# Strassen block products in the last channel products of an attention and MLP-mixer kernel

## The chip, the core and the metric

The kernel runs on one core of one Trainium2 chip. The metric is the device time of one execution in microseconds; lower is better. On the core the engines run side by side, each with a queue that it works off in order: PE (matrix products, with PEld loading the stationary operand), DVE (vector), ACT (scalar), POOL and SP, the last two here only issuing transfers.

## The reference

```python
scores = (q @ k.T) / sqrt(64)                    # q, k, v: 8 batches, 12 heads, 448 rows, 64 wide
attn = maximum(scores, 0) ** 2 / 448
x = (attn @ v) laid out as 8 x 448 x 768         # heads side by side
h = maximum(x.T @ w_tok1, 0) @ w_tok2            # mixing along the 448 rows, 256 wide inside
u = x + h.T
out = u + maximum(u @ w_ch1, 0) @ w_ch2          # the two channel products, 768 -> 1536 -> 768
```

Inputs and output are float32; the kernel multiplies in bf16 and accumulates in float32.

## The kernel before

**Steps.** A step s (0 to 23) is four heads of one batch, three steps to a batch. For each step q, k and v are loaded by POOL (`ld`), q and k are transposed (by PE for the first ten steps, later by a copy on DVE, `i`, and a transposing transfer of SP, `x`), and seven score blocks follow: `S{s}.{c}` on PE, two evictions with a rectifier `r` on ACT or DVE, a squaring `q` on DVE (L426), and the value product `V{s}.{c}` (L443), which adds up over the seven blocks. `xe` evicts it, `xd` transposes it by a transfer, `t1` and `rt`, then `t2` and `u` (L500, DVE) do the token mixing and leave a 128-channel slice of u in `uTs`, 6 x 896 columns for a pair of batches. `ub` (SP) transposes u a second time into `u_sbs`, for the residual at the end.

**Channel products.** For each batch b and each of twelve 128-column blocks e of w_ch1, `C1.{b}.{e}` is six matmuls of 448 columns in one of the eight PSUM banks (L521), evicted with a rectifier by ACT (`c1e`, L250) into `r2s`. For each pair of batches p and each of its seven 128-row tiles t, `C2.{p}.{t}.{i}` is twelve matmuls of 384 columns (L569) for each half i of the output row; DVE adds u (`c2e`, L576) into one of three output buffers, and SP stores the tile in two transfers (`st`, L559). The very last tile is made in three parts of 384, 256 and 128 columns.

**Order.** `ORDER` is one long list, written ahead of time, of every operation with its PSUM banks (a digit each) or its engine (A for ACT, D for DVE). Each engine works off its own operations in the order of this list, whatever becomes ready first; the framework adds the waits between engines, from the regions that instructions read and write. The list puts channel products of earlier batches between the score and value blocks, which alone would leave PE waiting for ACT and DVE.

**What the change touches.** The buffers (`raws`, `sides`, `kqTs`, `sqs`, `xTs`, `r1s`, `outs`), `channel2` (L544) with its stores, the loop over batches at the end (L595) and the part of `ORDER` from the last score blocks on.

Of the kernel before, what the change touches and what calls it, by code (L numbers as in the profile page):

```python
# [172 lines left out]
C1.5.4:3 c1e5.10:A q21.3:D q21.6:D t2.18.1:5 c1e5.4:A q22.4:D t1.19.0:2 u18.1:D V21.0:41 rt19.0:A ub6.1  # L173
S22.6:06 S23.0:73 V21.1 r22.6.0:A r22.6.1:D V21.2 S22.5:52 r23.0.0:A V21.3 r23.0.1:D S23.1:06 r22.5.0:A V21.4
r22.5.1:D V21.5 S23.2:73 r23.1.0:A V21.6 q23.0:D r23.1.1:A S23.3:52 C1.5.2:0 q22.5:D r23.2.0:A r23.2.1:A
r23.3.0:D r23.3.1:A t2.18.0:6 q23.1:D c1e5.2:A t2.19.1:7 q23.2:D C2.2.2.0:3 u18.0:D u19.1:D ub6.0 xe21.0:A
xe21.1:D q23.3:D C1.5.9:5 xd21 c2e2.2.0:D q22.6:D S22.2:20 c1e5.9:A S22.3:67 ub6.3 S22.0:41 r22.2.0:A
r22.2.1:D t1.20.0:3 r22.0.0:A r22.0.1:D r22.3.0:A C1.5.3:5 r22.3.1:D rt20.0:A q22.0:D t2.19.0:2 q22.2:D
c1e5.3:A V23.0:04 q22.3:D V22.0:16 V22.1 S23.6:73 u19.0:D V23.1 V23.2 r23.6.0:A V22.2 r23.6.1:D ub6.2 V22.3
S23.4:52 V22.4 q23.6:D V23.3 r23.4.0:A V22.5 S23.5:73 r23.4.1:A C2.2.1.0:5 r23.5.0:A r23.5.1:D q23.4:D q23.5:D  # L180
C1.5.0:2 c2e2.1.0:D t2.20.1:7 c1e5.0:A t2.20.0:3 u20.1:D V22.6 V23.4 u20.0:D V23.5 xe22.0:A ub6.5 V23.6
xe22.1:D C1.5.6:5 xe23.0:A xe23.1:D xd22 C1.6.8:2 c1e5.6:A ub6.4 t1.21.0:7 c1e6.8:A C1.6.0:3 rt21.0:A xd23
C1.5.8:1 c1e6.0:A C2.2.0.0:6 c1e5.8:A t1.22.0:0 c2e2.0.0:D C1.6.4:4 rt22.0:A C1.6.7:5 c1e6.4:A t1.23.0:2
c1e6.7:A t2.21.0:7 C1.5.1:3 u21.0:D ub7.0 t2.22.1:1 c1e5.1:A C1.6.2:6 u22.1:D ub7.3 C1.6.3:0 c1e6.2:A
t2.21.1:4 c1e6.3:A C1.6.11:5 u21.1:D ub7.1 rt23.0:A C1.5.11:7 c1e6.11:A t2.23.1:3 c1e5.11:A C1.6.1:1 u23.1:D
ub7.5 C2.2.1.1:6 c1e6.1:A t2.22.0:0 c2e2.1.1:D C1.6.10:4 u22.0:D st15.0 st15.64 t2.23.0:2 c1e6.10:A ub7.2
# [5 lines left out]
st22.64 C1.7.3:0 C2.2.3.0:4 c1e7.3:A C2.2.4.1:6 c2e2.3.0:D st17.0 st17.64 C2.2.6.1:7 c2e2.4.1:D st18.0 st18.64
C2.3.5.0:0 c2e2.6.0:D c2e2.6.1:D C2.3.2.0:4 st20.0 st20.64 c2e3.0.0:D c2e3.0.1:D C2.3.3.1:6 st21.0 st21.64
C2.3.3.0:1 c2e3.2.1:D c2e3.2.0:D st23.0 C2.3.4.0:7 st23.64 c2e3.3.0:D c2e3.3.1:D st24.0 C2.3.5.1:2 c2e3.4.0:D
st24.64 C2.3.4.1:3 c2e3.5.0:D c2e3.5.1:D st26.0 st26.64 C2.3.6.0:5 c2e3.4.1:D st25.0 st25.64 C2.3.6.1:4
c2e3.6.0:D st27.0.0 C2.3.6.2:1 st27.0.64 c2e3.6.1:D st27.1.0 c2e3.6.2:D st27.1.64 st27.2.0 st27.2.64
"""


# [1 line left out]
def kernel(ctx: ExitStack, tc: tile.TileContext, q: bass.AP, k: bass.AP, v: bass.AP, moe_w_tok1: bass.AP, moe_w_tok2: bass.AP, moe_w_ch1: bass.AP, moe_w_ch2: bass.AP, out: bass.AP):  # L201
    nc = tc.nc
    B, H, S, D = q.shape
# [20 lines left out]
    xTs = [sbuf.tile([128, 2, SP], BF16, name=f'xT{i}') for i in range(NX)]  # L224
# [23 lines left out]
    def relu(o, out, ps):  # L248
        if o.on == 'ACT':
            nc.scalar.activation(out, ps, AF.Relu)  # L250
# [293 lines left out]
    def channel2(bb, t):  # L544
        r2 = r2s[bb % 2]
        n = bb * NT + t
        out_sb = outs[n % NO]
        last = n == 4 * NT - 1
        parts = [(0, 3), (3, 5), (5, 6)] if last else [(0, 3), (3, 6)]
        rows = out[2 * bb:2 * bb + 2].rearrange('b (p c) m -> b c p m', c=KC)  # L550
        (b0, r0), (b1, r1) = (divmod(2 * t, KC), divmod(2 * t + 1, KC))
        pieces = [(slice(0, 64), rows[b0, r0]), (slice(64, 128), rows[b1, r1])]

        def store(name, cols, deps):
            for p, dst in pieces:
# [4 lines left out]
                w = 1.29 / len(pieces) * (cols.stop - cols.start) / DM  # L560
                st.setdefault(n, []).append(add(Op(f'st{name}.{p.start}', 'SP', emit_st, deps)))
        for i, (g0, g1) in enumerate(parts):
            cols = slice(g0 * 128, g1 * 128)
            size = (g1 - g0) * 128

            def emit(o, cols=cols, size=size):
                o.ps = bank(o, 0, 'm2_ps')
                for e in range(EC):
                    nc.tensor.matmul(o.ps[:, :size], lhsT=r2[:, e, t * 128:(t + 1) * 128], rhs=wc2[:, e, cols], start=e == 0, stop=e == EC - 1)  # L569
            deps = [c1e[2 * bb + h, e] for h in range(2) if (t <= HT if h == 0 else t >= HT) for e in range(EC)]  # L570
            deps += list(wc2_ops.values())
            u = Op(f'C2.{bb}.{t}.{i}', 'PE', emit, deps, banks=1)
            c2[bb, t, i] = add(u)

            def evict(o, u=u, cols=cols, size=size, g0=g0, g1=g1):
                nc.vector.tensor_tensor(out=out_sb[:, cols].rearrange('n (g d) -> n g d', d=128), in0=u.ps[:, :size].rearrange('n (g d) -> n g d', d=128), in1=u_sbs[bb % 2][:, g0:g1, t, :], op=ALU.add)  # L576
# [70 lines left out]
```

## Time and profile before

| | |
|---|---|
| median of 3 runs | 361.92 us (360.82 to 362.55) |
| span of the profiled execution | 360.1 us |
| its own time beside the span | not among the numbers; the median of the runs is 1.8 us above the span |
| PE busy | 351.5 us, 98% of the span |
| DVE, ACT busy | 243.8 and 190.0 us, 68% and 53% |
| mean granted TensorE clock | 0.994 of full speed |

The span runs from the first to the last instruction of the profiled execution. Busy time of an engine is the time in which at least one of its instructions ran; the durations of DVE and ACT instructions overlap by some tens of nanoseconds where they follow each other directly, so the distance between two starts, not the duration, is what one costs in a full queue. In a chain of waits, each piece is followed back to what released it.

### The profile page before, as it was taken

The numbers are of one execution on the slowest core, as the hardware profiler recorded it, in microseconds if no ns is written. First come the engines' busy times: TensorE is split into PE (matmuls) and PEld (weight loads), VectorE is DVE, ScalarE is ACT, GpSimd is POOL, SyncE is SP. The second block draws the span as 40 slices with busy tenths as digits, with TensorE's granted clock in tenths as the row PEclk, the third lists the DMA queues.
The fourth block names the chain that finished last, engine by engine and source line by source line (L and its number), as shares of the span: only waits on it lengthen the run. The fifth ranks groups of instructions, "written<-read, shape, count | busy, mean of one in ns | idle before, by whom it ended". The sixth has DMA issues, their size and how long they took to land.

```text
span 360.1 us, 8713 instructions
## 1 busy us (share of the span) xinstructions
PE 351.5 (98%) x3543; PEld 196.9 (55%) x3543; DVE 243.8 (68%) x457; ACT 190.0 (53%) x392; POOL 92.0 (26%) x157
## 2 busy tenths in 40 slices
PE   7799999999999999999999999999999999999995
PEld 3456555565555545655555555555556555555563
DVE  3999995978686898989986879788970211101342
ACT  3999996546654667537665637367644432110000
POOL 9985313530650333303330523010000000000000
PEclk9899999999999999999999999999999999999999
DMA  8999999999999989999999999974213231103555
GB/s 150 182 181 165 186 190 200 133 172 220 91 194 130 166 173 199 180 187 146 174 205 190 111 176 159 231 140 87 53 23 71 44 89 44 46 0 87 129 134 133
DMA packets 98297, 50.17 MB, mean 139 GB/s; under 512 B 71440, under 2 KB 94800, under 8 KB 98256
## 3 DMA queue, kind: packets, MB, share of 16 engines
q1 hardware_dynamic: 72880, 27.93, 45.2%
q0 software_dynamic: 25136, 21.47, 44.4%
q8 instruction: 28, 0.46, 0.5%
q10 hardware_dynamic: 240, 0.20, 0.2%
q14 instruction: 13, 0.11, 0.1%
HBM read 43.38 MB, written 11.01 MB: 151 GB/s over the span
## 4 chain that ended last, share of the span: by engine, by line
PE 93%; DVE 2%; ACT 2%; DMA 1%; issue 0%; SPq 0%
PE m_ps L521 31%; PE m_ps L569 31%; PE sc_ps L416 9%; PE acc_ps L443 9%; PE t_ps L487 6%; PE h_ps L496 5%; ACT sq L250 1%; DMA side<-in_q_dram 1%; PE kqT_ps L373 1%; DVE sq L426 1%; PE x_ps L478 1%; DVE sq L252 1%; DVE kqT L258 0%; ACT kqT L256 0%; SPq L325 0%
## 5 line engine op out<-in xcount | busy, mean ns | idle before, releaser
L250 ACT ACTIVATE sq<-sc_ps 128x448 bf16<-128x448 f32 x232 | 110.6, 570 | 29.7 <-PE sc_ps L416 28.5
L521 PE MATMUL m_ps<-uT_sb,wc 128*128 128x448 bf16 x576 | 118.7, 353 | 0.0
L569 PE MATMUL m_ps<-wc,r_sb 128*128 128x384 bf16 (+2 forms) x684 | 114.6, 323 | 0.0
L250 ACT ACTIVATE r_sb<-m_ps 128x448 bf16<-128x448 f32 x96 | 52.8, 551 | 88.5 <-PE m_ps L521 88.1
L426 DVE TENSOR_TENSOR sq<-sq 128x896 bf16<-128x896 bf16 x168 | 97.0, 617 | 0.6
L569 PEld LDWEIGHTS <-r_sb 128*128 128x128 bf16 x684 | 65.8, 98 | 45.8 <-issue 3.1
L521 PEld LDWEIGHTS <-wc 128*128 128x128 bf16 x576 | 54.5, 98 | 54.1 <-issue 7.3
L576 DVE TENSOR_TENSOR out_sb<-m_ps,u_sb 128x384 f32<-128x384 f32 (+2 forms) x57 | 30.9, 549 | 72.5 <-PE m_ps L569 65.2
L252 DVE TENSOR_SCALAR sq<-sc_ps 128x448 bf16<-128x448 f32 x104 | 60.6, 617 | 12.2 <-PE sc_ps L416 11.9
L272 POOL DMA_DIRECT2D v_raw<-in_v_dram x48 | 29.0, 608 | 121.4 <-PE sc_ps L416 76.7
L416 PE MATMUL sc_ps<-kqT 64*64 64x448 bf16 x672 | 54.7, 361 | 0.7 <-DVE kqT L258 0.2
L443 PE MATMUL acc_ps<-sq,v_raw 64*64 64x448 bf16 x672 | 49.2, 357 | 1.8 <-DVE sq L426 1.8
L500 DVE TENSOR_TENSOR uT_sb<-h_ps,xT 128x448 bf16<-128x448 f32 x48 | 28.8, 618 | 17.3 <-PE h_ps L496 17.2
L272 POOL DMA_DIRECT2D k_raw<-in_k_dram x48 | 29.4, 625 | 13.7 <-DMA wc<-in_moe_w_ch_dram 6.4
L416 PEld LDWEIGHTS <-kqT 64*64 64x64 bf16 x672 | 20.6, 107 | 20.3 <-issue 11.8
L272 POOL DMA_DIRECT2D q_raw<-in_q_dram x46 | 28.3, 629 | 7.4 <-PE m_ps L521 4.2
L443 PEld LDWEIGHTS <-v_raw 64*64 64x64 bf16 x672 | 20.9, 108 | 15.6 <-issue 6.7
L487 PE MATMUL t_ps<-x_sb,wt 128*128 128x256 bf16 (+1 forms) x216 | 25.4, 261 | 0.0
L250 ACT ACTIVATE r_sb<-t_ps 128x512 bf16<-128x512 f32 (+1 forms) x26 | 15.0, 584 | 19.1 <-PE t_ps L487 19.0
L496 PE MATMUL h_ps<-wt,r_sb 128*128 128x448 bf16 x96 | 24.3, 353 | 0.0
L487 PEld LDWEIGHTS <-wt 128*128 128x128 bf16 x216 | 18.9, 98 | 7.3 <-issue 1.8
L455 DVE TENSOR_SCALAR xT<-acc_ps 128x448 bf16<-128x448 f32 x24 | 14.7, 617 | 0.2 <-PE acc_ps L443 0.2
(35 smaller groups left out, 103.3 us busy)
## 6 DMA issues: line engine op xcount, KB each, us to landing
out_dram<-out_sb SPq DMA_DIRECT2D x54, 192.0 KB, 3.4
k_raw<-in_k_dram POOLq DMA_DIRECT2D x48, 112.0 KB, 6.1
v_raw<-in_v_dram POOLq DMA_DIRECT2D x48, 112.0 KB, 5.0
q_raw<-in_q_dram POOLq DMA_DIRECT2D x46, 112.0 KB, 6.6
wc<-in_moe_w_ch_dram POOLq DMA_DIRECT2D x6, 768.0 KB, 16.9
u_sb<-uT_sb SPq DMA_TRANSPOSE x48, 4.6
side<-in_q_dram SPq DMA_DIRECT2D x2, 224.0 KB, 3.8
kqT<-side SPq DMA_TRANSPOSE x28, 6.3
```

Of the source, the lines that this page charges most:

```text
L250: nc.scalar.activation(out, ps, AF.Relu)
L252: nc.vector.tensor_scalar(out=out, in0=ps, scalar1=0.0, scalar2=None, op0=ALU.max)
L272: nc.gpsimd.dma_start(out=raws[t][s % NR][64 * half:64 * (half + 1)], in_=src[b, h0:h0 + 2].rearrange('e (p c) d -> p e (c d)', c=KC))
L416: nc.tensor.matmul(o.ps[e][64 * half:64 * (half + 1), :S], lhsT=lhsT, rhs=rhs, start=True, stop=True, skip_group_check=True)
L426: sq_ops[s, c] = [add(Op(f'q{s}.{c}', 'DVE', lambda o: nc.vector.tensor_tensor(out=buf, in0=buf, in1=buf, op=ALU.mult), ev))]
L443: nc.tensor.matmul(o.ps[half][64 * e:64 * (e + 1), :S], lhsT=r[rows, e, c * D:(c + 1) * D], rhs=sq[rows, e, :], start=c == 0, stop=c == KC ...
L487: nc.tensor.matmul(o.ps[:, j, :], lhsT=wt1[:, c, j * 128:(j + 1) * 128], rhs=x_sb[:, p0:p1, c, :], start=c == 0, stop=c == 3)
L496: nc.tensor.matmul(o.ps[:, :S], lhsT=r1[:, j, a * 128:(a + 1) * 128], rhs=wt2[:, j, :], start=j == 0, stop=j == JC - 1)
L500: nc.vector.tensor_tensor(out=uTs[bb % 2][:, 2 * i + a, off:off + S].rearrange('n (c p) -> n c p', c=KC), in0=t2.ps[:, :S].rearrange('n (p ...
L521: nc.tensor.matmul(ps[:, :S], lhsT=wc1[:, g, e * 128:(e + 1) * 128], rhs=uT[:, g, off:off + S], start=g == 0, stop=g == CC - 1)
L569: nc.tensor.matmul(o.ps[:, :size], lhsT=r2[:, e, t * 128:(t + 1) * 128], rhs=wc2[:, e, cols], start=e == 0, stop=e == EC - 1)
L576: nc.vector.tensor_tensor(out=out_sb[:, cols].rearrange('n (g d) -> n g d', d=128), in0=u.ps[:, :size].rearrange('n (g d) -> n g d', d=128 ...
```

## The change

A matrix product in 2 x 2 blocks needs eight block products; Strassen's scheme (in Winograd's form) needs seven, and sums of blocks ahead of and behind them. The changed kernel uses it in two places. For the last pair of batches (p = 3) the first channel product is made of seven block products for each of six pairs of column blocks (`fast1`: `M1.3.{e}.{name}`, three matmuls of 448 columns each). For the last two pairs (p = 2 and 3), the second channel product is made so for the tiles t = 0, 1, 2 together with 4, 5, 6 (`fast2`: `M2.{p}.{t}.{name}`, six matmuls of 384 columns each, giving two tiles); tile 3 stays as it was.

New operations: `w2` and `w1`, sums of blocks of the two weights (8 of 128x1152 and 12 of 128x768 bf16, DVE); `tu`, sums of blocks of u (4 of 128x1344, DVE); `s1`, copies of a PSUM bank to float32 in SBUF (18, ACT), after which more is accumulated onto the same bank; `d1`, which join a copy and a bank (24 of 128x448, DVE); `z1`, the rectifier in place on 128x896 (12: 5 on DVE, 7 on ACT); `h2` and `h3`, sums of blocks of its result (24 each of 128x384 bf16, DVE); `d2`, which add u and the products into an output buffer (48 of 128x384, DVE, in place of 24 `c2e`). The `c1e` of the last two batches go (24, ACT). The sums lie in one large tile, `arena`, which the loads, transposes and squares of the attention use before, and the output buffers grow from three to five, two of them where `xTs` was. The order is unchanged up to `u18.1`, in the middle of the attention's last steps, and new from there.

```diff
+FAST1, FAST2 = ({3}, {2, 3})
+TILES = [*range(14), 14, 18, 15, 19, 16, 20, 17, 21, 25, 22, 26, 23, 27, 24]
...
 C1.5.4:3 c1e5.10:A q21.3:D q21.6:D t2.18.1:5 c1e5.4:A q22.4:D t1.19.0:2 u18.1:D
...
+w2.0.1:D t2.18.0:4 w2.0.0:D
+ub6.1 rt19.0:A t1.20.0:1 u18.0:D w2.1.0:D t2.19.1:0 ub6.0 rt20.0:A t2.19.0:6 u19.1:D V21.0:73 V21.1 u19.0:D
...
+tu3.3:D M1.3.0.1:6 M1.3.1.1:0 M1.3.1.5:5 s1.3.0.1:A M1.3.1.2:7 s1.3.1.1:A M1.3.0.2:4 M1.3.1.6 M1.3.0.6
...
+h3.2.2:D d2.2.1.22a:D d2.2.0.22b:D M2.2.1.4:6 d2.2.0.21b:D d2.2.1.12a:D st18.64 M2.2.1.3 d2.2.1.21a:D st18.0
+M2.2.1.7 d2.2.1.12b:D st15.64 M2.2.2.2:0 d2.2.1.22b:D st15.0 d2.2.1.21b:D M2.2.2.1:7 st19.64 st19.0 M2.2.2.5:2
...
+st22.64 M2.3.2.7 d2.3.1.22b:D st22.0 d2.3.1.21b:D M2.3.2.3 d2.3.2.22b:D st26.0 d2.3.2.21b:D st26.64 C2.3.3.0:4
+d2.3.2.12b:D st27.0 st23.0 st23.64 C2.3.3.1:3 st27.64 c2e3.3.0:D st24.0.64 C2.3.3.2:5 st24.0.0 c2e3.3.1:D
+st24.1.0 c2e3.3.2:D st24.2.0 st24.2.64 st24.1.64
...
+    arena = sbuf.tile([128, 3 * NR * 896 + NSIDE * 2 * KC * 128 + NQ * 4 * S + NSQ * 896], BF16, name='arena')
...
+    def weight_sums(k, w, dst, step, deps):
+        w11, w12, w21, w22 = w
...
+            if k == 2:
+                x = one(0, dst[0], w12, w11, ALU.subtract, [])
+                y = one(1, dst[1], w22, dst[0], ALU.subtract, x)
+                one(2, dst[2], w22, w12, ALU.subtract, [])
+                one(3, dst[3], dst[1], w21, ALU.subtract, y)
+            else:
+                x = one(0, dst[0], w21, w22, ALU.add, [])
...
+    def fast1(p):
...
+        t1_ = add2(f'tu{p}.0', tu[:, 0], u12, u11, ALU.subtract, early[:3] + late[:3] + gone)
+        t2_ = add2(f'tu{p}.1', tu[:, 1], u22, tu[:, 0], ALU.subtract, [t1_] + late[3:])
...
+        for e in range(EC // 2):
...
+            m1 = product('1', A(0, lo), u11, early)
+            m2 = product('2', A(1, lo), u21, early)
+            a1, k1 = snap(0, m1, '1')
+            c11 = join('11', r2[:, e, :S], k1, a1, m2, ALU.add)
+            m6 = product('6', s2w, tu[:, 1], [t2_, a1] + ws_ops[1, 1], m1)
+            a2, k2 = snap(1, m6, '2')
+            m7 = product('7', A(0, hi), tu[:, 2], [t3_, a2] + ws_ops[1, 2], m1)
+            a3, k3 = snap(2, m7, '3')
+            m5 = product('5', s1w, tu[:, 0], [t1_] + ws_ops[1, 0])
+            c22 = join('22', r2[:, EC // 2 + e, S:], k3, a3, m5, ALU.add)
+            m3 = product('3', s4w, u22, late + [c22] + ws_ops[1, 3], m5)
+            c12 = join('12', r2[:, e, S:], k2, a2, m3, ALU.add)
+            m4 = product('4', A(1, hi), tu[:, 3], [t4_])
+            c21 = join('21', r2[:, EC // 2 + e, :S], k3, a3, m4, ALU.subtract)
...
+    def fast2(p):
...
+            x = add2(f'h{p}.{e}.0', s1[:, e], h21, h22, ALU.add, deps)
+            y = add2(f'h{p}.{e}.1', s2[:, e], s1[:, e], h11, ALU.subtract, [x])
+            w = add2(f'h{p}.{e}.2', h21, h11, h21, ALU.subtract, [x])
+            z = add2(f'h{p}.{e}.3', s4[:, e], h12, s2[:, e], ALU.subtract, [y])
...
+            m2 = product('2', r2[:, e_hi, te], wc2[:, e_hi, c_lo], ce[6:] + w2)
+            m1 = product('1', r2[:, e_lo, te], wc2[:, e_lo, c_lo], ce[:6] + w2)
+            f11 = take('11a', t, c_lo, m2, [], True)
+            g11 = take('11b', t, c_lo, m1, [f11], False)
+            m5 = product('5', s1[:, :, ts], ws2[0], done[0] + ws_ops[2, 0])
+            f22 = take('22a', q, c_hi, m5, [], True)
+            m6 = product('6', s2[:, :, ts], ws2[1], done[1] + [g11] + ws_ops[2, 1], m1)
+            f12 = take('12a', t, c_hi, m6, [], True)
+            m3 = product('3', s4[:, :, ts], wc2[:, e_hi, c_hi], done[3] + [f22] + w2, m5)
+            g12 = take('12b', t, c_hi, m3, [f12], False)
+            m4 = product('4', r2[:, e_hi, to], ws2[3], co[6:] + ws_ops[2, 3])
+            f21 = take('21a', q, c_lo, m4, [], True, ALU.subtract)
+            m7 = product('7', r2[:, e_lo, to], ws2[2], done[2] + [f12] + ws_ops[2, 2], m1)
+            g22 = take('22b', q, c_hi, m7, [f22], False)
+            g21 = take('21b', q, c_lo, m7, [f21], False)
```

A product called with a last argument (`m1`, `m5`) adds onto that product's bank and so comes after the instruction that has read it; a list in brackets names what an operation waits for.

More of the change, by code (lines that the diff above doesn't have):

```diff
@@ L172 @@
 S22.4:52 c1e4.0:A S21.3:41 S21.6:06 r22.4.0:A r22.4.1:D C1.5.10:7 r21.3.0:A r21.3.1:D r21.6.0:A r21.6.1:D
[L173 to L186, printed above, removed]
@@ L192 @@
[L192 to L196, printed above, removed]
+C1.5.4:3 c1e5.10:A q21.3:D q21.6:D t2.18.1:5 c1e5.4:A q22.4:D t1.19.0:2 u18.1:D w2.0.1:D t2.18.0:4 w2.0.0:D
@@ L223 @@
     ident = sbuf.tile([128, 128], BF16, name='ident')
-    xTs = [sbuf.tile([128, 2, SP], BF16, name=f'xT{i}') for i in range(NX)]
+    xT_all = sbuf.tile([128, NX, 2, SP], BF16, name='xT')
+    xTs = [xT_all[:, i] for i in range(NX)]
     wt1 = sbuf.tile([128, 4, DT], BF16, name='wt1')
@@ L542, in channel1, with out_free, stores @@
         return u
-    def channel2(bb, t):
-        r2 = r2s[bb % 2]
+    out_slot = {n: k % 3 for k, n in enumerate(TILES[:14])} | {n: int(k) for n, k in zip(TILES[14:], '01201234012340')}
+    before = {n: ([m for m in TILES[:i] if out_slot[m] == out_slot[n]] or [None])[-1] for i, n in enumerate(TILES)}
+    def out_free(n):
+        m = before[n]
+        if m is not None:
+            return st[m]
+        return [ue[s, a] for s in range(NS - 3, NS) for a in range(2)] if out_slot[n] > 2 else []
+    def stores(bb, t):
         n = bb * NT + t
-        out_sb = outs[n % NO]
-        last = n == 4 * NT - 1
+        out_sb = outs[out_slot[n]]
+        last = n == TILES[-1]
         parts = [(0, 3), (3, 5), (5, 6)] if last else [(0, 3), (3, 6)]
@@ L561, in store, with channel2 @@
                 st.setdefault(n, []).append(add(Op(f'st{name}.{p.start}', 'SP', emit_st, deps)))
+        return out_sb, parts, store
+    def channel2(bb, t):
+        r2 = r2s[bb % 2]
+        n = bb * NT + t
+        last = n == TILES[-1]
+        out_sb, parts, store = stores(bb, t)
         for i, (g0, g1) in enumerate(parts):
@@ L571, in channel2 @@
             deps += list(wc2_ops.values())
-            u = Op(f'C2.{bb}.{t}.{i}', 'PE', emit, deps, banks=1)
+            u = Op(f'C2.{bb}.{t}.{i}', 'PE', emit, deps, banks=1, size=size)
             c2[bb, t, i] = add(u)
@@ L576, in evict @@
                 nc.vector.tensor_tensor(out=out_sb[:, cols].rearrange('n (g d) -> n g d', d=128), in0=u.ps[:, :size].rearrange('n (g d) -> n g d', d=128), in1=u_sbs[bb % 2][:, g0:g1, t, :], op=ALU.add)
-            deps = [u] + [ub[2 * bb + (t >= HT), g] for g in range(g0, g1)] + st.get(n - NO, [])
-            c2e[bb, t, i] = add(Op(f'c2e{bb}.{t}.{i}', 'DVE', evict, deps))
+            deps = [u] + [ub[2 * bb + (t >= HT), g] for g in range(g0, g1)] + out_free(n)
+            c2e[bb, t, i] = add(Op(f'c2e{bb}.{t}.{i}', 'DVE', evict, deps, size=size))
             if last:
@@ L582, in channel2, with add2, one @@
             store(f'{n}', slice(0, DM), [c2e[bb, t, 0], c2e[bb, t, 1]])
+    def add2(name, dst, x, y, op, deps, **kw):
+        return add(Op(name, 'DVE', lambda o: nc.vector.tensor_tensor(out=dst, in0=x, in1=y, op=op), deps, **kw))
+    ws_ops = {}
+    def weight_sums(k, w, dst, step, deps):
+        w11, w12, w21, w22 = w
+        wt = []
+        n = dst[0].shape[1] // step
+        for i in range(n):
+            c = slice(i * step, (i + 1) * step)
+            def one(j, d, x, y, op, more):
+                o = add2(f'w{k}.{j}.{i}', d[:, c], x[:, c], y[:, c], op, deps + more)
+                ws_ops.setdefault((k, j), []).append(o)
+                return [o]
+            if k == 2:
[5 more added lines that the diff above has]
+                x = one(0, dst[0], w21, w22, ALU.add, [])
+                y = one(1, dst[1], dst[0], w11, ALU.subtract, x)
+                one(2, w21, w11, w21, ALU.subtract, x)
+                one(3, dst[2], w12, dst[1], ALU.subtract, y)
@@ new lines, in fast1, with product, emit, snap @@
+    def fast1(p):
+        uT, r2, tu = (uTs[p % 2], r2s[p % 2], uTs[1 - p % 2].rearrange('p g n -> p (g n)').rearrange('p (k g n) -> p k g n', k=4, g=3))
+        u11, u12, u21, u22 = (uT[:, g:g + 3, off:off + S] for g in (0, 3) for off in (0, S))
+        early, late = ([[ue[s, a] for s in range(GS * b, GS * (b + 1)) for a in range(2)] for b in (2 * p, 2 * p + 1)])
+        gone = [c1[b, e] for b in (2 * p - 2, 2 * p - 1) for e in range(EC)] + [ub[b, g] for b in (2 * p - 2, 2 * p - 1) for g in range(CC)]
+        t1_ = add2(f'tu{p}.0', tu[:, 0], u12, u11, ALU.subtract, early[:3] + late[:3] + gone)
+        t2_ = add2(f'tu{p}.1', tu[:, 1], u22, tu[:, 0], ALU.subtract, [t1_] + late[3:])
+        t3_ = add2(f'tu{p}.2', tu[:, 2], u22, u12, ALU.subtract, late + gone)
+        t4_ = add2(f'tu{p}.3', tu[:, 3], tu[:, 1], u21, ALU.subtract, [t2_] + early[3:])
+        free2 = [c2.get((p - 2, t, i)) for t in range(NT) for i in range(2)]
+        for e in range(EC // 2):
+            lo, hi = (slice(e * 128, (e + 1) * 128), slice(DC // 2 + e * 128, DC // 2 + (e + 1) * 128))
+            def product(name, lhs, rhs, deps, on=None, first=False, more=False):
+                o = Op(f'M1.{p}.{e}.{name}', 'PE', None, deps, banks=0 if on else 1, holder=on)
+                def emit(o):
+                    o.ps = on.ps if on else bank(o, 0, 'm1_ps')
+                    for g in range(3):
+                        nc.tensor.matmul(o.ps[:, :S], lhsT=lhs[:, g], rhs=rhs[:, g], start=g == 0 and not on, stop=g == 2, skip_group_check=True)
+                o.emit = emit
+                return add(o)
+            def snap(i, u, name):
+                k = snap_n[0] % len(snaps)
+                snap_n[0] += 1
+                o = add(Op(f's1.{p}.{e}.{name}', 'ACT', lambda o: nc.scalar.activation(snaps[k], u.ps[:, :S], AF.Copy), [u] + snap_free[k], reads=[u]))
+                snap_free[k] = []
+                return o, k
+            def join(name, dst, k, s_, u, op, *more):
+                o = Op(f'd1.{p}.{e}.{name}', 'DVE', lambda o: nc.vector.tensor_tensor(out=dst, in0=snaps[k], in1=u.ps[:, :S], op=op), [s_, u, *free2, *more], reads=[u])
+                snap_free[k].append(o)
+                return add(o)
+            A = lambda i, c: wc1[:, 3 * i:3 * i + 3, c]
+            s1w, s2w, s4w = (w[:, :, lo] for w in ws1)
+            m1 = product('1', A(0, lo), u11, early)
[12 more added lines that the diff above has]
+            c21 = join('21', r2[:, EC // 2 + e, :S], k3, a3, m4, ALU.subtract)
+            for name, e_, cs in (('a', e, [c11, c12]), ('b', EC // 2 + e, [c21, c22])):
+                o = add(Op(f'z1.{p}.{e}.{name}', 'ACT', lambda o, e_=e_: relu(o, r2[:, e_], r2[:, e_]), cs))
+                c1e[2 * p, e_] = c1e[2 * p + 1, e_] = o
```

140 lines of the change are left out of this document (125 added, 15 removed).

## The prediction

> **What bounds the kernel now.** I read the page's busy shares and chain first, then the busy time by stretch, because the change touches only the last 110 us, and then the spacing of instructions in the timeline.
>
> ```profile
> span 360.1 us, 8713 instructions
> PE 351.5 (98%) x3543; PEld 196.9 (55%) x3543; DVE 243.8 (68%) x457; ACT 190.0 (53%) x392; POOL 92.0 (26%) x157
> ...
> PE 93%; DVE 2%; ACT 2%; DMA 1%; issue 0%; SPq 0%
> ```
>
> PE is the bound: busy for 98% of the span and 93% of the chain that ended last.
>
> ```profile
> core 0: us, PE busy (x) PEld busy (x) DVE busy (x) ACT busy (x) POOL busy (x), PEclk, DMA share, GB/s
> 27.00:45.00 18.00, 18.00 (x374) 10.09 (x376) 17.93 (x36) 17.63 (x40) 7.87 (x12) 1.00 1.21 175
> 250.26:268.57 18.31, 18.31 (x198) 9.86 (x199) 15.89 (x30) 10.94 (x23) 0.00 (x0) 1.00 0.18 37
> 268.57:317.00 48.43, 48.43 (x282) 27.22 (x279) 8.07 (x15) 16.08 (x31) 0.00 (x0) 1.00 0.26 57
> 250.26:356.14 105.88, 105.88 (x726) 61.02 (x726) 34.52 (x63) 28.48 (x55) 0.00 (x0) 1.00 0.30 70
> ```
>
> The old and new order part after `u18.1`. The product issued just ahead of it, `t1.19.0`, ends at 250.26, and from there to its last matmul PE never stops: 105.88 of 105.88 us. DVE works only 34.5 us of that stretch. So fewer matmuls shorten the kernel one for one, as long as DVE, which gets nearly all the new work, keeps up. The row of 27 to 45 us shows that PE, DVE and ACT can be full at the same time in this kernel.
>
> **What PE saves.** Rates come from pieces of the chain that hold one kind of matmul:
>
> ```profile
> 309.49 3.90 PE m_ps L569 x24
> 313.39 4.54 PE m_ps L521 x24
> ...
> 351.89 4.27 PE m_ps L569 x38
> 356.16 0.02 issue
> 356.19 0.29 DVE out_sb L576
> ```
>
> A matmul of 448 columns takes 4.54/24 = 0.189 us, one of 384 columns 3.90/24 = 0.1625 us. The first channel product of the last pair had 24 x 6 = 144 matmuls and gets 6 x 7 x 3 = 126: 18 fewer, 3.40 us. In the second product, six tiles of a pair had 6 x 2 x 12 = 144 and get 3 x 7 x 6 = 126; two pairs, 36 fewer, 5.85 us. Together 9.25 us. With PE still full, its last matmul would end at 356.16 - 9.25 = 346.9. No matmul is slower by itself: shapes stay.
>
> **What DVE gets.** What an instruction costs in a full queue is the distance between starts:
>
> ```profile
> 28.16 1.15 DVE L426 TENSOR_TENSOR sq<-sq 128x896 bf16<-128x896 bf16 x2
> 29.23 0.62 DVE L500 TENSOR_TENSOR uT_sb<-h_ps,xT 128x448 bf16<-128x448 f32 x1
> ...
> 31.89 0.75 DVE L258 COPY x_sb<-x_ps 128x512 bf16<-128x512 bf16 x2
> 32.56 0.61 DVE L426 TENSOR_TENSOR sq<-sq 128x896 bf16<-128x896 bf16 x1
> ...
> 230.46 0.61 DVE L394 COPY side<-k_raw 128x896 bf16<-128x896 bf16 x1
> 230.98 0.61 DVE L394 COPY side<-q_raw 128x896 bf16<-128x896 bf16 x1
> ...
> 249.54 0.62 DVE L500 TENSOR_TENSOR uT_sb<-h_ps,xT 128x448 bf16<-128x448 f32 x1
> ...
> 338.60 1.02 DVE L576 TENSOR_TENSOR out_sb<-m_ps,u_sb 128x384 f32<-128x384 f32 x2 [1.38 <-DMA out_dram<-out_sb]
> ```
>
> Two squares of 896 bf16 from 28.16 to 29.23 are 0.533 us each, and so is an instruction of 448 elements that reads a bank (1.15 for two, less its own 0.617). Two copies of 512 take 32.56 - 31.89 = 0.67, 0.335 each; two outputs of 384 take 1.02, 0.465 each after the last one's 0.556. All lie on one line: 0.067 us, plus 1.04 us per thousand elements from a bank in float32, plus half of that per thousand of bf16. By it the sums cost: `h` (384 bf16) 0.267, `w1` (768) 0.467, `w2` (1152) 0.667, `tu` (1344) 0.767. `d1` (448, a bank) is 0.533, `d2` (384, a bank) 0.467. No row shows the rectifier `z1` on 896 bf16 from SBUF to SBUF: its nearest rows are the copies of 512 at 0.335 and the square at 0.533, which I take as its ends; I use 0.52, the distance of the two `side` copies, which have its size and go from SBUF to SBUF as it does.
>
> The order then says where PE meets DVE. For each product that waits for a DVE instruction I added up DVE's queue from 250.07 (`u18.1` at 249.54 plus 0.533) to that instruction, and PE's remaining work from the product on. The latest end comes from `M2.2.1.7`, which waits for `d2.2.1.12a`. Up to there DVE has 148 instructions: 57 of 0.533 (12 squares, 7 rectifiers, 11 `u`, 3 `xe`, 24 `d1`) 30.4; all 48 `h` 12.8; 8 `w2` 5.3; 12 `w1` 5.6; 4 `tu` 3.1; 14 `c2e` and `d2` 6.5; 5 `z1` 2.6: 66.3 us. So it ends at 316.4, or 316.5 with the 0.09 by which a duration exceeds the distance. Behind it PE has 29 products of 6 x 0.1625 = 28.3 and the last tile:
>
> ```profile
> 354.20 0.56 DVE L576 TENSOR_TENSOR out_sb<-m_ps,u_sb 128x384 f32<-128x384 f32 x1 [1.39 <-PE m_ps L569]
> 355.51 0.42 DVE L576 TENSOR_TENSOR out_sb<-m_ps,u_sb 128x256 f32<-128x256 f32 x1 [0.75 <-PE m_ps L569]
> 356.19 0.29 DVE L576 TENSOR_TENSOR out_sb<-m_ps,u_sb 128x128 f32<-128x128 f32 x1 [0.25 <-PE m_ps L569]
> ```
>
> Its parts take 1.95, 1.31 and 0.68, 3.9 together. 316.5 + 28.3 + 3.9 = 348.7: DVE, not PE, sets the pace for the first 66 us, and takes 1.8 of the 9.25 us back. From there on DVE is light (48 `d2` in all against 42 products of 0.975) and PE sets the pace.
>
> **What lies between.** Each pair of column blocks adds round trips: product, ACT's copy, more onto the same bank, DVE's join. Seven products are 4.0 us of PE; ACT needs three copies (448 elements, 0.55 us each by the row below, 0.44 apart in the run of eight) and about one rectifier, some 2.2 us, so ACT isn't the bound; and it loses 24 `c1e` for 18 copies and 7 `z1`.
>
> ```profile
> L250 ACT ACTIVATE r_sb<-m_ps 128x448 bf16<-128x448 f32 x96 | 52.8, 551 | 88.5 <-PE m_ps L521 88.1
> 250.81 3.60 ACT L250 ACTIVATE sq<-sc_ps 128x448 bf16<-128x448 f32 x8
> ```
>
> The order interleaves two blocks, so that a product waits for a copy issued at least two products (1.1 us) earlier; a copy takes 0.55 and some 0.2 to start. What remains is DVE standing still because the head of its queue waits for PE. Bounds: 0.4% of 66 us, 0.3 us, as in the full stretch from 27 to 45 us, and 4 us, some half of the idle share in the row 250.26:268.57 (2.4 of 18.3), where DVE didn't set the pace. I take 1.5, nearer the full stretch. PE's last matmul then ends at 350.2.
>
> **Buffers and stores.**
>
> ```profile
> out_dram<-out_sb SPq DMA_DIRECT2D x16, 192.0 KB, 2.6
> 335.00:345.00 10.00, 10.00 (x63) 6.06 (x62) 3.89 (x8) 0.00 (x0) 0.00 (x0) 1.00 0.61 157
> ```
>
> A half tile lands 2.6 us after its issue. The tightest buffer in the new order is that of tile 19, which waits for tile 14, stored some 4.6 us earlier by DVE's queue: covered; with slower stores PE would wait by the difference. At the end four tiles are finished within 3 us. 157 GB/s at a share of 0.61 is 257 GB/s at most, 0.77 us per half tile: eight halves are 6.1 us, from 6.1 us ahead of the last matmul on, so they are through before the last part lands. Before, the span ended 360.1 - 356.16 = 3.9 us behind the last matmul; I take 4.2. Span 354.4. The median lies 1.8 above the span (361.92 - 360.1; no own time of the profiled execution is given): **356.2 us**, 5.7 less.
>
> **The rivals.**
>
> *PE's own floor.* DVE is never late: 346.9 + 3.9 + 1.8 = 352.6, say 353. It needs cheaper `z1` and fuller cover than I count. 0.07.
>
> *DVE takes its whole durations.* If each instruction waits for the one in front of it to end (sums read sums, `d2` b reads what a wrote), the 148 cost 0.617 for 0.533, some 0.085 more each: 12.6 us. Time 368.8, slower. If half of them do: 362.5, no change. Against it: the pairs above that follow at 0.533; and the order puts other work between most dependent sums. 0.05 each. The Trainium skill, page "VectorE: DVE Perf Modes", section "The DRAIN you can't avoid", says the next instruction doesn't start until the pipe is empty, and advises fewer instructions. By that rule this is the case that comes, for any DVE queue; the row of two squares in 1.15 us, not 1.23, disagrees.
>
> *Sums at half the rate (ends on the other side).* The only bf16 sum-like row, the square, reads the same tile twice. If two different operands go at the rate of the float32 rows, `h` costs 0.2 more, `w2` 0.6, `w1` 0.4, `tu` 0.7: 9.6 + 4.8 + 4.8 + 2.8 = 22 us, all ahead of `d2.2.1.12a`. Time 378.2. It turns from gain to loss once the sums take 5.7 us more than counted, a quarter of that. For it: no row excludes it. Against it: the square is issued as an instruction with two inputs, and gains the bf16 rate. 0.07. The same page, in its perf-mode tier table, gives two-input instructions on bf16 in SBUF twice the float32 rate; no run here shows it with two different inputs, and by that rule this case has no chance.
>
> *The change doesn't do what it says.* Buffers carved from one tile could make loads wait for one another, and gaps on PE could lower its clock.
>
> ```profile
> 281.86 2.43 PE L521 MATMUL m_ps<-uT_sb,wc 128*128 128x448 bf16 x12
> 282.06 0.62 DVE L500 TENSOR_TENSOR uT_sb<-h_ps,xT 128x448 bf16<-128x448 f32 x1 [0.89 <-PE h_ps L496]
> 9.00:18.00 9.00, 6.95 (x143) 4.00 (x144) 8.38 (x16) 8.28 (x18) 8.24 (x15) 0.81 1.25 182
> ```
>
> Against the first: `u21.1` writes columns of `uTs` at 282.06 while matmuls ahead of it in the order read other columns of the same tile; it didn't wait. Against the second: the clock fell to 0.81 where PE was busy 77%; here 96.6 of some 100 us would be. At 0.81 for 66 us it costs 66 x 0.23 = 15 us, 371. 0.03 for both.
>
> **How the numbers follow.** Forecast 0.73, its own range 353.5 to 360.3: the idle time's ends (0.3 and 4 for 1.5) give 355.0 and 358.7, 1 us more for the stores' end 359.7, and the runs' spread (360.82 to 362.55 around 361.92) and a cheaper `z1` the rest. With the floor below it and the half-way case above, 353.0 to 362.5 leaves out less than 2 in 10. A measurement can tell about 0.5%, 1.8 us: faster (under 360.1) is the forecast but 0.02 at its end, and the floor, 0.78; the same is that end and the half-way case, 0.07; slower 0.05 + 0.07 + 0.03 = 0.15.
>
> **What would show it.** Right: 3489 matmuls; the `h` rows near 0.27 apart and `w2` near 0.67; DVE almost full from 250 to 316 us with PE waiting for it by some 3 us in all, and PE full afterwards; the last matmul near 350, the span's end 4 us later. Wrong: sums twice as long, DVE starts a duration apart, PE waiting for DVE behind 320 us, a clock under 1.00, or a difference ahead of 250 us, where nothing should move.

## The result, and the profile after

The changed kernel takes 355.62 us (median of 4 runs, 355.15 to 355.79) against 361.53 for the kernel before beside it; the ratio is 0.983, 95% interval 0.981 to 0.985. Forecast were 356.2 us. The profiled execution took 355.15, with a span of 353.4, 1.75 less than its time. First the page:

```profile
span 353.4 us, 8749 instructions
PE 343.5 (97%) x3489; PEld 191.3 (54%) x3489; DVE 294.8 (83%) x580; ACT 193.8 (55%) x395; POOL 91.8 (26%) x157
...
PE 91%; DVE 5%; DMA 1%; ACT 0%; issue 0%; SPq 0%
```

54 matmuls are gone, PE is 8.0 us less busy, DVE 51 us more; DVE now has 5% of the chain. The stretches from where the order is new (PE, PEld, DVE, ACT and POOL busy in each; then clock, DMA share and GB/s):

```profile
250.00:270.00 20.00, 19.40 (x203) 9.55 (x201) 20.00 (x37) 13.55 (x28) 0.00 (x0) 1.00 0.36 58
270.00:283.00 13.00, 13.00 (x81) 7.70 (x80) 13.00 (x28) 3.95 (x8) 0.00 (x0) 1.00 0.43 76
283.00:317.00 34.00, 34.00 (x193) 18.67 (x192) 33.59 (x88) 14.88 (x23) 0.00 (x0) 1.00 0.13 31
317.00:349.00 32.00, 31.34 (x205) 19.38 (x203) 19.42 (x37) 0.00 (x0) 0.00 (x0) 1.00 0.47 128
```

DVE is full from 250 to 316, as forecast, and 61% busy after that. PE is full too, but for 0.6 us, up to its last matmul. The clock is 1.00 in all four stretches. Pieces of the chain from 257 us on, each with its start, length and count:

```profile
257.78 1.24 PE m_ps L562 x6
259.02 0.31 PE sc_ps L457 x4
...
259.53 0.19 PE sc_ps L457 x4
...
267.02 1.13 PE m_ps L562 x6
...
279.52 21.10 PE m_ps L683 x111
300.62 2.93 PE m_ps L748 x18
303.55 0.57 PE m_ps L683 x3
304.11 0.97 PE m_ps L748 x6
305.09 2.27 PE m_ps L683 x12
307.36 37.05 PE m_ps L748 x228
344.41 3.94 PE m_ps L624 x36
```

All 252 block-product matmuls of 384 columns and 126 of 448 run without a gap: from 279.36, the last row of the timeline below, to the last matmul's end at 344.41 + 3.94 = 348.35 are 69.0 us, and by the rates of before they need 126 x 0.189 + 252 x 0.1625 + 3.94 = 68.7.

```profile
255.79 1.30 PE L562 MATMUL m_ps<-uT_sb,wc 128*128 128x448 bf16 x6 [0.60 <-DVE uT_sb L541]
...
279.36 1.30 PE L683 MATMUL m_ps<-uT_sb,wc 128*128 128x448 bf16 x6
```

The last matmul was forecast at 350.2 and PE's own floor was 346.9. So 1.45 us are lost to the floor, nearly all ahead of 279.36. One wait takes 0.6: `C1.5.1` needs the bank that `u20.1` reads, and DVE has the sums w2.1.1 and w2.3.0 right ahead of it. Most of the rest is no wait but the change between score or value products (64x64) and 128x128 products: behind such a change six matmuls take 1.24 in the chain instead of 1.13, and a score group of four takes 0.31 instead of 0.19. From 250 us to the first block product the new order goes there and back seven times, the old order, in the same part, four times; three more at 0.23 are an estimated 0.7 us.

DVE's queue, at the point where the forecast put its end:

```profile
308.53 0.37 DVE L639 TENSOR_TENSOR arena<-r_sb 128x384 bf16<-128x384 bf16 x1
308.80 0.56 DVE L761 TENSOR_TENSOR out_sb<-out_sb,m_ps 128x384 f32<-128x384 f32 x1
...
312.00 1.71 DVE L639 TENSOR_TENSOR r_sb<-r_sb 128x384 bf16<-128x384 bf16 x6
...
315.00 1.03 DVE L759 TENSOR_TENSOR out_sb<-u_sb,m_ps 128x384 f32<-128x384 bf16 x2
...
317.15 1.02 DVE L761 TENSOR_TENSOR out_sb<-out_sb,m_ps 128x384 f32<-128x384 f32 x2 [0.42 <-PE m_ps L748]
```

`d2.2.1.12a`, the first of the two at 315.00, ends near 315.5; forecast were 316.4 to 316.5. `M2.2.1.7` must start 28.3 + 3.94 us ahead of 348.35, at 316.1, so DVE is some half a microsecond early, and the next waits are DVE's, for PE.

**The end.** The span ends 353.4 - 348.35 = 5.05 us behind the last matmul, 3.9 before. SP's queue (start and length of a merged row, count at its end):

```profile
342.10 2.55 SPq L608 DMA_DIRECT2D out_dram<-out_sb  x4
344.75 2.89 SPq L608 DMA_DIRECT2D out_dram<-xT  x4
347.74 3.17 SPq L608 DMA_DIRECT2D out_dram<-out_sb  x3
```

Eleven stores queue there one behind another, each taking SP 0.47 to 0.97 us; the last one ends at 350.9, though its data are in the buffer at 348.7 (the last `c2e` starts at 348.38 and takes 0.29).

### The profile page after: what moved, and what is told of

Its sections match the earlier page's. It is cut to its first block, busy times and chain, and to the rows that moved or that the text cites. A ratio compares the mean times of both kernels' runs of the same rounds, so it can differ in the third digit from the quotient of the medians.

```text
span 353.4 us, 8749 instructions
## 1 busy us (share of the span) xinstructions
PE 343.5 (97%) x3489; PEld 191.3 (54%) x3489; DVE 294.8 (83%) x580; ACT 193.8 (55%) x395; POOL 91.8 (26%) x157
## 4 chain that ended last, share of the span: by engine, by line
PE 91%; DVE 5%; DMA 1%; ACT 0%; issue 0%; SPq 0%
PE m_ps L562 24%; PE m_ps L624 18%; PE m_ps L748 12%; PE sc_ps L457 10%; PE acc_ps L484 9%; PE m_ps L683 7%; PE t_ps L528 6%; PE h_ps L537 5%; DVE arena L467 2%; DMA arena<-in_q_dram 1%; PE kqT_ps L414 1%; DVE uT_sb L541 1%; DVE arena L639 1%; PE x_ps L519 1%; DVE arena L293 1%; DVE arena L299 1%
## 5 line engine op out<-in xcount | busy, mean ns | idle before, releaser
L291 ACT ACTIVATE arena<-sc_ps 128x448 bf16<-128x448 f32 x234 | 112.0, 573 | 28.8 <-PE sc_ps L457 27.6
L467 DVE TENSOR_TENSOR arena<-arena 128x896 bf16<-128x896 bf16 x168 | 97.0, 618 | 0.5
L562 PE MATMUL m_ps<-uT_sb,wc 128*128 128x448 bf16 x432 | 89.5, 353 | 0.6 <-DVE uT_sb L541 0.6
L293 DVE TENSOR_SCALAR arena<-sc_ps 128x448 bf16<-128x448 f32 x102 | 59.5, 617 | 9.7 <-PE sc_ps L457 9.6
L624 PE MATMUL m_ps<-wc,r_sb 128*128 128x384 bf16 (+2 forms) x396 | 66.6, 322 | 0.0
L313 POOL DMA_DIRECT2D arena<-in_v_dram x48 | 29.3, 620 | 118.3 <-PE sc_ps L457 75.2
L457 PE MATMUL sc_ps<-arena 64*64 64x448 bf16 x672 | 54.4, 361 | 0.7 <-DVE arena L299 0.2
L484 PE MATMUL acc_ps<-arena 64*64 64x448 bf16 x672 | 49.2, 358 | 1.8 <-DVE arena L467 1.8
L313 POOL DMA_DIRECT2D arena<-in_k_dram x48 | 29.6, 629 | 14.8 <-DMA wc<-in_moe_w_ch_dram 6.5
L457 PEld LDWEIGHTS <-arena 64*64 64x64 bf16 x672 | 20.5, 107 | 20.7 <-issue 12.6
L484 PEld LDWEIGHTS <-arena 64*64 64x64 bf16 x672 | 20.8, 108 | 15.5 <-issue 6.8
```

The costliest lines, as they stand in the source:

```text
L313: nc.gpsimd.dma_start(out=raws[t][s % NR][64 * half:64 * (half + 1)], in_=src[b, h0:h0 + 2].rearrange('e (p c) d -> p e (c d)', c=KC))
L457: nc.tensor.matmul(o.ps[e][64 * half:64 * (half + 1), :S], lhsT=lhsT, rhs=rhs, start=True, stop=True, skip_group_check=True)
L467: sq_ops[s, c] = [add(Op(f'q{s}.{c}', 'DVE', lambda o: nc.vector.tensor_tensor(out=buf, in0=buf, in1=buf, op=ALU.mult), ev))]
L484: nc.tensor.matmul(o.ps[half][64 * e:64 * (e + 1), :S], lhsT=r[rows, e, c * D:(c + 1) * D], rhs=sq[rows, e, :], start=c == 0, stop=c == KC ...
L562: nc.tensor.matmul(ps[:, :S], lhsT=wc1[:, g, e * 128:(e + 1) * 128], rhs=uT[:, g, off:off + S], start=g == 0, stop=g == CC - 1)
```

## The experiments

Two theories after this trace. *PE alone*: DVE looks full only because the order feeds it early; PE lost 0.6 us at one wait, some spacing, and 1.1 at the end. *Both*: PE and DVE are critical together up to the block products of pair 2, so that any longer DVE queue, or any idle time of DVE, comes back on PE. Since stalls early in a trace shift all that follows (in the first trace of e1 PE is busy for 60.6 of the 63 us from 27 to 90, in that of the changed kernel for all 63), the times of parts are taken from landmarks inside a trace: the first block product, the last matmul, the span's end.

**The changed kernel again.**

> The changed kernel unaltered, as the measure for the other three of this set. All theories: 355.6 us within 0.4, span 353.4 to 354.0, last matmul near 348.3, PE idle 0.6 us near 255.2.

355.21 us (354.06 to 356.6). The last matmul ends at 347.16 in a span of 352.3, 5.1 behind it; block products to last matmul 69.0 again.

**e1: half of the last stores on ACT's queue.**

```diff
-queue = nc.scalar if last and p.start else nc.sync
+queue = nc.scalar if p.start and (last or n in (22, 26, 23, 27)) else nc.sync
```

> Issues the second half of the four tiles ahead of the last one (22, 26, 23, 27) on ACT's queue instead of SP's. Theory (the end is held by SP's queue: eleven store issues from 342.1 on, the last at 350.4 though its data are ready at 348.7): the last issue moves to about 348.9 and the span's end follows the last matmul by 3.9 us instead of 5.1, so 1.0 to 1.2 us less, 354.5. Rival (the transfers themselves are the limit: 1.9 MB at the rate of the 16 DMA engines): no change, 355.6.

354.34 us, 0.9 less than the changed kernel beside it, and 354.78 in a second set. In that second trace (span 352.6, last matmul at 344.51 + 3.94 = 348.45), SP's queue:

```profile
342.20 1.90 SPq L602 DMA_DIRECT2D out_dram<-out_sb  x2
344.62 1.12 SPq L602 DMA_DIRECT2D out_dram<-xT  x2
347.08 2.29 SPq L602 DMA_DIRECT2D out_dram<-out_sb  x3
```

SP's queue ends at 349.4 instead of 350.9, and the span 4.15 us behind the last matmul (348.45) instead of 5.05. The transfers weren't the limit; SP's queue was, for these 0.9 us. The medians' ranges overlap, so the 0.9 rests on the two traces.

**e2: three sums of weights later.**

```diff
-... V21.4 w2.1.1:D V21.5 t2.20.1:5 w2.3.0:D ... w2.3.1:D ... w2.2.0:D
+... V21.4 V21.5 t2.20.1:5 ... w2.1.1:D w2.3.0:D w2.3.1:D w2.2.0:D
```

> Moves three of the eight sums of the second channel weight (w2.1.1, w2.3.0, w2.3.1; 2.0 us of DVE) from the last score blocks to behind them, ahead of w2.2.0; the DVE work in all up to d2.2.1.12a is the same. Theory (PE lost 0.6 us waiting for u20.1 behind these sums, and DVE reaches d2.2.1.12a 0.4 us ahead of PE's need): 0.4 to 0.6 us less, 355.1, the wait near 255 gone. Rival of the prediction (DVE's full queue up to d2.2.1.12a sets the pace, wherever its parts stand): no change, 355.6, PE waiting later instead.

356.35 us, 1.1 more than the changed kernel: both numbers expected were wrong. The trace, first two stretches as above, then the timeline:

```profile
250.00:270.00 20.00, 20.00 (x205) 9.71 (x203) 19.09 (x35) 13.84 (x29) 0.00 (x0) 1.00 0.39 64
270.00:283.00 13.00, 11.71 (x71) 6.60 (x70) 13.00 (x28) 3.37 (x6) 0.00 (x0) 1.00 0.31 62
```
```profile
281.93 0.85 DVE L633 TENSOR_TENSOR uT_sb<-uT_sb,uT_sb 128x1344 bf16<-128x1344 bf16 x1
282.83 1.88 PE L677 MATMUL m_ps<-uT_sb,arena 128*128 128x448 bf16 x9 [1.04 <-DVE uT_sb L633]
```

The wait near 255 is gone, PE is full up to 270 and reaches its first block product 0.6 us earlier, at 278.22 in a trace that runs 0.54 us ahead of the other up to 254. But DVE, with the sums out of its way, runs dry for 0.9 us there. The sums then stand ahead of `tu3.1` (the first row of the timeline), which starts 32.3 us behind the end of `u18.1` (its start plus 0.533) instead of 30.9, and the block products wait for it; from the first of them to the last matmul are 70.9 us, 1.9 more. In the changed kernel `tu3.1` had only 0.2 us of lead on the first product that reads it:

```profile
281.12 0.85 DVE L639 TENSOR_TENSOR uT_sb<-uT_sb,uT_sb 128x1344 bf16<-128x1344 bf16 x1
282.19 1.87 PE L683 MATMUL m_ps<-uT_sb,arena 128*128 128x448 bf16 x9
```

What DVE lost by standing still, PE paid later. That speaks for *both*, and the place that this edit hits is not `d2.2.1.12a` but `tu3.1`, 34 us earlier.

**e3: e1, e2 and the rectifiers of DVE on ACT.**

```diff
-z1.3.1.b:D z1.3.1.a:D z1.3.0.a:D z1.3.3.a:D z1.3.3.b:D
+z1.3.1.b:A z1.3.1.a:A z1.3.0.a:A z1.3.3.a:A z1.3.3.b:A
```

> Both edits above, and the five z1 that DVE has go to ACT (1.5 us of DVE's queue). Theory: the gains add up, 1.6 to 1.8 us less than the changed kernel, 353.9, since DVE's lead at d2.2.1.12a grows by 1.5. Rival for the z1 (an in-place rectifier takes 0.95 us on ACT against 0.39 on DVE, and the h sums wait for it): up to 0.6 us of new waits on PE between 283 and 300 us, 354.5.

358.08 us, 2.9 more than the changed kernel, and 1.7 more than e2 although the stores of e1 are in it. From the first block product to the last matmul are 73.3 us, 4.3 more than in the changed kernel. Taking 1.5 us off DVE's queue made it stand still longer: 2.9 of the 34 us from 283 to 317, against 0.4. ACT, DVE and PE there:

```profile
290.36 1.78 ACT L285 ACTIVATE r_sb<-r_sb 128x896 bf16<-128x896 bf16 x2
292.04 0.53 ACT L684 ACTIVATE wt<-m_ps 128x448 f32<-128x448 f32 x1
292.46 0.95 ACT L285 ACTIVATE r_sb<-r_sb 128x896 bf16<-128x896 bf16 x1
292.62 0.73 PE L677 MATMUL m_ps<-uT_sb,wc 128*128 128x448 bf16 x3 [0.79 <-ACT wt L684]
...
295.30 0.62 DVE L689 TENSOR_TENSOR r_sb<-x_sb,m_ps 128x448 bf16<-128x448 f32 x1 [1.40 <-ACT x_sb L684]
```

The copies of the banks queue behind the rectifiers on ACT, the joins on DVE and the products that add onto the bank wait for the copies. The rival was right in kind and far too small (0.6).

**e4 and e5: each half of the change alone.** In e4 the places of `M1` hold `C1.6` and `C1.7` groups, in e5 those of `M2` hold `C2` groups; sums, copies and joins of the part go.

```diff
-FAST1, FAST2 = ({3}, {2, 3})
+FAST1, FAST2 = (set(), {2, 3})   # e4
+FAST1, FAST2 = ({3}, set())      # e5
```

> The first channel product of the last pair done as before (24 groups of six matmuls in the places of the block products), the second by block products as in the change. Theory (PE sets the pace, 18 matmuls of 0.189 come back): 3.4 us more than the changed kernel, 359.0. Rival of the prediction (DVE sets the pace up to 316 us): DVE loses some 23 us of work, so part of the 3.4 is covered by DVE being no longer late: 1.6 us more, 357.2.

358.51 us (ratio to before 0.990, 0.987 to 0.993). The first group of pair 3 starts at 278.72 and the last matmul ends at 351.01: 72.3 us, 3.3 more than the 69.0 of the changed kernel. PE's 3.4 come back in full, though DVE is 22 us less busy in the whole kernel: the block products of this part cost PE nothing beyond their matmuls.

> The second channel product of both pairs done as before (24 groups of twelve matmuls), the first of the last pair by block products. Theory: 36 matmuls of 0.1625 come back, 5.85 us, less the 0.6 us that PE waited behind the sums of the second weight (they are gone) and up to 0.8 at the end, as tiles finish one by one: 360.2 to 361. Rival (DVE sets the pace): 5.85 less 1.8, 359.7, with no difference at the end.

360.59 us (ratio to before 0.995, 0.992 to 0.998). From 278.79 to the last matmul at 353.53 are 74.7 us, 5.75 more, of 5.85 expected. The 0.6 us wait is gone in this trace; the 1.24 and 0.31 us behind a change of product size stay, though DVE has 2.7 of the 20 us from 250 on free, so they aren't waits for it. So the two parts add up, and the second is worth nearly two thirds.

**e6 and e7: 3.2 us more of DVE, early and late.**

```diff
+    for i in range(16):
+        add2(f'extra{i}', warm[:, :256], warm[:, :256], warm[:, 256:], ALU.add, [])
```

> The changed kernel with 16 more DVE instructions of 128x256 bf16 (0.20 us each by the line 0.067 + 0.52 per thousand elements: 3.2 us) between the d1 of the first channel product, ahead of d2.2.1.12a. Theory (DVE reaches d2.2.1.12a 0.4 us ahead of PE's need): 2.8 us more, 358.4. Rival of the prediction (DVE already sets the pace): 3.2 more, 358.8. Third (DVE looks full only because it is fed early, with several us to spare): no change.

358.39 us. Block products to last matmul take 351.98 - 280.11 = 71.9 us, 2.9 more for 16 instructions that each take 0.20 to 0.21 from start to start (3.3). So DVE had 0.4 us to spare, and no more: *PE alone* falls. The 16 instructions stand behind `tu3.1`, so there is a second tight stretch behind it. PE waits there for joins and a copy between 294 and 303 us (1.7 us in all), and its last wait is the one that the forecast named, `M2.2.1.7` for `d2.2.1.12a` (the first of the two at 319.00):

```profile
319.00 1.01 DVE L754 TENSOR_TENSOR out_sb<-u_sb,m_ps 128x384 f32<-128x384 bf16 x2
319.61 1.14 PE L743 MATMUL m_ps<-arena,r_sb 128*128 128x384 bf16 x6 [0.16 <-DVE out_sb L754]
```

> The same 16 instructions behind 317 us, between the d2 of the last blocks, where DVE is busy 61%. All theories but one: no change (within 0.3), 355.6. If each d2 is on PE's path there (products that add onto a bank wait for it), up to 3.2 us more.

354.74 us (ratio to before 0.981); block products to last matmul 69.2, against 69.0. Behind 317 us DVE has room.

**e8 and e9: six sums of weights on POOL.** Each pair of POOL's instructions here computes the second half twice and leaves out the first; their number, size and place are those of a whole sum.

```diff
-o = add2(f'w{k}.{j}.{i}', d[:, c], x[:, c], y[:, c], op, deps + more)
+o = add(Op(f'w{k}.{j}.{i}', 'POOL', lambda o: nc.gpsimd.tensor_tensor(...), deps + more))   # k == 2 and j > 0
```

> The stores as in e1, and six of the eight sums of the second channel weight (w2.1, w2.2, w2.3) computed by POOL, which stands still from about 240 us on, instead of DVE (4.0 us of DVE's queue). Theory (DVE's queue is as critical as PE's, since idle time of DVE came back as a later wait one for one in e2; DVE's lead ahead of the block products is 0.2 to 0.4 us): the 0.6 us wait near 255 goes and doesn't come back, and 0.3 more between 283 and 317; with the store's 0.9 it gives 1.5 to 1.9 us less than the changed kernel, 353.5. Rival (POOL and DVE hinder each other while both read SBUF, or POOL is too slow for M2.2.0.4): DVE's instructions next to POOL's get longer, 354.5 to 357.

> The same six sums on POOL, with the stores of the changed kernel. Theory: 0.6 to 0.9 us less than the changed kernel, 354.5, and 1.0 more than e8. Rival (hindrance): 355.5 or more; the difference to e8 stays 1.0 under both.

359.42 us (e8) and 360.78 (e9). Neither e1 nor the changed kernel ran beside them; by the ratios to the kernel before, 0.993 and 0.996 against 0.978 for e1 and 0.983, they take some 5 us more each time. The granted clock from 250 to 270 us was 0.91 in e9 but 1.00 in e8, so it isn't the cause. DVE in e8, with POOL below it:

```profile
255.40 0.61 DVE L535 TENSOR_TENSOR uT_sb<-h_ps,xT 128x448 bf16<-128x448 f32 x1
255.93 2.74 DVE L461 TENSOR_TENSOR arena<-arena 128x896 bf16<-128x896 bf16 x1
258.59 1.67 DVE L287 TENSOR_SCALAR arena<-sc_ps 128x448 bf16<-128x448 f32 x3
260.19 7.66 DVE L461 TENSOR_TENSOR arena<-arena 128x896 bf16<-128x896 bf16 x5
```
```profile
255.82 5.07 POOL L645 TENSOR_TENSOR arena<-arena,wc 128x1152 bf16<-128x1152 bf16 x2
260.85 5.45 POOL L645 TENSOR_TENSOR arena<-wc 128x1152 bf16<-128x1152 bf16 x2
```

A square, 0.62 us alone, takes 2.74; five take 7.66 instead of 2.76. Instructions with an input from a bank (`u`, the rectifiers) keep their 0.6. The hindrance, not the wait for POOL's results, is what costs: PE's waits between 250 and 320 us are for squares and rectifiers of the score blocks, 4.9 us in all, and none is for POOL. The Trainium skill, page "SBUF — State Buffer", section "Who interferes with whom", says that a DVE instruction with two SBUF inputs and a GpSimd instruction that reads SBUF shut each other out, and that one with at most one SBUF input, outside the modes in which DVE takes both ports, doesn't; these rows agree on both.

**e10: one swap and one rectifier.**

```diff
-t2.20.1:5 w2.3.0:D t2.20.0:2 ... V21.6 u20.1:D ... r23.4.0:D
+t2.20.1:5 u20.1:D w2.3.0:D t2.20.0:2 ... V21.6 ... r23.4.0:A
```

> The stores as in e1; DVE does u20.1 ahead of w2.3.0 instead of behind it, so that PE's 0.6 us wait near 255 goes without DVE standing still; and one rectifier of the last score blocks (r23.4.0, 0.53 us) goes from DVE to ACT. Theory (PE and DVE are both critical up to the block products, DVE with 0.2 us of lead): DVE's queue is 0.53 shorter, so PE gets its 0.6 but 0 to 0.1: 0.5 to 0.6 us less than e1, and no new wait at the first block products. Rival (DVE's order doesn't matter beyond that one wait and the rest is spacing of PE's own): the same 0.6. Second rival (ACT's queue delays xe22.0 and so the last token mixing): 0 to 0.4 us more than e1.

> e1 again, as the measure for e10: 354.4 us within 0.5, span 4.1 us behind the last matmul.

354.09 us against 354.78 for e1 beside it; but the two traces, which start the new part within 0.02 us of each other, differ by 0.15 at the last matmul (348.30 and 348.45). The wait near 255 goes, as expected, without DVE standing still; PE is 0.67 us ahead at `C1.5.1`, 0.35 at the next groups and 0.07 at the first block product. So 0.6 was not kept. The two halves of the edit weren't tried apart: the last of the lead goes where `t2.21.1` follows a score block whose bank `r23.4.0` now empties from ACT, which would be a wait for ACT, as in the second rival; the rest goes earlier, in waits of the score blocks for DVE. The fastest kernels are e1 and e10, ratios to before 0.978 and 0.978 in their sets, 0.980 for e1 in the second; e10 isn't told apart from e1.

## Why the prediction was right

*PE's saving, 9.25 us.* Right. The matmuls number 3489, and e4 and e5 gave each part back: 3.3 and 5.75 us of the 3.4 and 5.85 counted.

*DVE's price by the distance of starts.* Right: six `h` from 312.00 to 313.61 are 0.27 each as forecast, an `h` is followed after 0.27 by a `d2` at 308.80, and the sums of two different operands run at the bf16 rate (1152 elements in 0.75 us, the second row below). That settles two rivals. The Trainium skill (page "VectorE: DVE Perf Modes", section "The DRAIN you can't avoid") says that the next instruction doesn't start until the pipe is empty, and in the same paragraph that one that is not held starts earlier; so "for any DVE queue" in the prediction is broader than the page. By its first sentence alone six `h` would have taken an estimated 6 x 0.36 = 2.2 us; they took 1.71. Three groups of DVE's new instructions, with busy time and mean ns of one:

```profile
L639 DVE TENSOR_TENSOR arena<-wc,arena 128x768 bf16<-128x768 bf16 x3 | 1.6, 554 | 0.0
L639 DVE TENSOR_TENSOR arena<-wc,arena 128x1152 bf16<-128x1152 bf16 x2 | 1.5, 748 | 0.0
L293 DVE TENSOR_SCALAR r_sb<-r_sb 128x896 bf16<-128x896 bf16 x5 | 1.9, 395 | 0.0
```

*One term was mis-sized:* `z1`. It was taken at 0.52, between ends of 0.335 and 0.533, and two follow each other 0.31 apart (0.70 for two below, 0.395 for one above), under the lower end:

```profile
288.34 0.70 DVE L293 TENSOR_SCALAR r_sb<-r_sb 128x896 bf16<-128x896 bf16 x2
```

The five come 1.1 us cheaper than counted, and `d2.2.1.12a` came 0.9 us ahead of its forecast. So DVE wasn't 1.8 us late at that point but half a microsecond early. The other `z1`, on ACT, were counted as some 0.55 and take 0.95 each; ACT's work for a pair of column blocks is then 2.6 us instead of 2.2, still under PE's 4.0.

*DVE sets the pace.* Not in this run. The forecast named some 3 us of PE waiting for DVE as a sign; PE waited 0.6, far from the place that it named. DVE was half a microsecond short of pacing PE there: in e6, with 3.3 us more of DVE, PE's last wait is the named one.

*DVE's idle time, 1.5 us.* Too much: DVE was busy for all of the 65.5 us from 250 to 315.5. What PE lost instead, 1.45 us against its floor, lies mostly at the last score blocks, for which the sum has no term. And the working kept only the place with the latest end: e2 shows that `tu3.1`, with 0.2 us of lead, is tight as well.

*The end, 4.2 us.* Too little: 5.05. The working weighed the transfers, and not that each store takes SP 0.47 to 0.97 us to issue; e1 shows that it is the queue.

The three misses partly cancel: the last matmul came 1.85 us early (1.1 for `z1` and 0.75 for the idle time less what PE itself lost), the end took 0.85 more, and the median lies 2.2 us above the profiled span instead of the 1.8 assumed. That leaves 0.6, in part by luck, and it says less for the single terms than it seems.

*The rivals.* PE's floor was missed by 1.45 us. Buffers carved from one tile cost nothing that shows: in the stretch from 27 to 45 us PE is busy 18.00, as before:

```profile
27.00:45.00 18.00, 18.00 (x374) 10.00 (x375) 18.00 (x35) 17.63 (x40) 7.52 (x12) 1.00 1.22 165
```

An output buffer that was still being stored held DVE for 0.86 us ahead of 319.03, without a wait of PE. From 250 us on the clock stayed at 1.00.

## What to carry to other kernels

Fewer matmuls shorten a kernel that PE bounds only as far as another engine can take the extra work at the same pace: add up each engine's queue by the distance of starts up to the first instruction that the other waits for, at every such place and not just the one with the latest end. When two engines are full together, order is worth as much as work: moving 2 us of DVE's work, or giving 1.5 us of it to ACT, made the kernel slower by 1.1 and by a further 1.7 us or more, because here an engine that stood still once in a full queue didn't get that time back. Look at the last transfers' issue queue apart from their bytes; a second issuing engine gave 0.9 us here for one changed line.

## What the runs showed of the hardware

POOL working in SBUF isn't free for DVE: a square of SBUF data beside it took 2.74 us instead of 0.62, while DVE instructions that read a bank kept their 0.6. Behind an in-place rectifier of 896 bf16 from SBUF to SBUF DVE starts its next instruction after 0.31 us; two copies of the same size into `side` started 0.52 apart before. On PE each change between 64x64 and 128x128 products cost 0.11 to 0.12 us.
